# Leaving out the eleven filler products behind the first product of chunk 0's join

## The chip, the cores and the metric

The kernel runs on one core of a Trainium2 chip. The core has five engines that take instructions from queues of their own: PE (TensorE, matrix products; its weight loads are listed as PEld), DVE (VectorE), ACT (ScalarE), POOL (GpSimd) and SP (SyncE, which here only issues DMAs). The metric is the device time of one execution in microseconds. Before the change three runs took 508.95, 509.15 and 509.38 us, with a median of 509.15 us.

## The reference

A delta-rule attention over 4 batches, 8 heads, 768 positions of 48 channels, and behind it, on the heads put together to 384 channels, a layer norm and an MLP with a residual:

```python
k_n = k / (np.linalg.norm(k, axis=-1, keepdims=True) + 1e-06)
for t in range(S):
    kt, vt, bt = (k_n[:, :, t], v[:, :, t], beta[:, :, t, None])
    y[:, :, t] = np.einsum('bhd,bhde->bhe', q[:, :, t], state)
    v_old = np.einsum('bhde,bhd->bhe', state, kt)
    state = state + bt[:, :, :, None] * np.einsum('bhd,bhe->bhde', kt, vt - v_old)
...
xn = (x - mu) / np.sqrt(var + 1e-06) * g_ln
ch = np.maximum(xn @ w_ch1, 0.0) @ w_ch2
return (x + ch).astype(np.float32)
```

Inputs and output are float32, apart from the two weight matrices, which reach the kernel as float64 and are converted there to float32.

## The kernel before

**Tiling.** The 768 positions are cut into 12 chunks of 64. Within a chunk the recurrence is solved as a triangular system. Its inverse is made on DVE: `rows_inverse` (L823) does two chunks at a time by row elimination, a multiplication (L849) and a subtraction (L856) per row, 31 rows. Before it starts it scales the Gram matrix by `db_b`, which needs the inputs beta in `beta_b` (L834, L838), and POOL puts the diagonal into `xb` (L835). Chunk 0 has a way of its own that is done sooner: `rows_near` inverts blocks of 16 rows, and `near_join` (L801) joins two of them by two products on PE, both on line L812, each of 128 matmuls of 32 by 32. Between the two, ACT copies the first product's result with a sign (L815); after the second, DVE puts it into place (L819).

**The recurrence.** `recur(c)` (L875) computes for a chunk `u` in three products (L908) with an ACT copy into `u` after the first and the third (L914) and a DVE subtraction after the second (L912), then the outputs (L919, copied by ACT at L956), and the update of the state (L929, which ACT copies into `s_all` at L940 in chunk 0). The layer norm follows: statistics on DVE (L962, L963), the root on ACT (L968), scaling on DVE (L974), transposes on PE (L1006), and for chunk 0 the gain on ACT (L1022) and DVE (L1012). Products of the keys and queries with the state (L886) open the next chunk.

**The MLP.** `mlp(c)` multiplies the normed chunk by the two weight matrices. In chunks 0 to 2 the first matrix is done at L1184 and chunk 0's second at L1206; later chunks use schemes with fewer products (L1100, L1281). All of these are PE work, and from some 67 us on they fill PE.

**Loads.** SP issues nearly all loads in one queue, in the order of its instructions: keys (`kr`, `tb`), queries (`tb`), `v`, and beta in eight pieces. One that waits holds all behind it. The function that issues them is `dma` (L370; the trace names its line L373). ACT issues the loads of the weights, which ACT, DVE and POOL convert (L514, L519, L522, L532).

**Order.** The function records 2783 steps, each with its engine. `ORDER`, a tuple of step numbers, says in which order they are issued; `in_this_order` binds each engine to that order, and the DMAs of SP and ACT to one another. What a step waits for comes from the tiles that it reads and writes.

**The filler products.** `zeros` multiplies `nought` by a column of `nought` that is repeated 256 times, into columns of the PSUM bank `f0`; nothing reads the result:

```python
def zeros():
    nc.tensor.matmul(f_[0][:, 256:512], nought, nought[:, 0:1].to_broadcast([128, 256]))
for _ in range(WARM):
    add("PE", 0.44, zeros, FK[0], [], np=2, arr=0.44, name="warm", after=["nought"])
```

With `WARM = 26` these are steps 62 to 87; the trace names their line L1364. `nought` is the first 128 columns of the tile `u`. `Line.emit` asks of every step that the steps it depends on were issued before it, except for steps named "warm", which may stand anywhere or be left out. On the chip each is two weight loads and two matmuls, since a float32 product takes two passes.

Of the kernel before, what the change touches and what calls it, by code (L numbers as in the profile page):

```python
# [57 lines left out]
def pool(n):  # L58
# [13 lines left out]
    346, 72, 80, 86, 183, 64, 54, 203, 223, 123, 213, 179, 126, 191, 220, 206, 194, 215, 14, 226, 184, 202, 296, 297, 329, 328, 199, 219, 298, 227,  # L72
    82, 340, 228, 197, 710, 196, 208, 299, 62, 44, 198, 185, 331, 356, 343, 344, 385, 330, 386, 204, 192, 217, 300, 229, 231, 186, 230, 233, 234, 235,
    49, 83, 63, 347, 236, 221, 301, 302, 304, 303, 305, 360, 306, 322, 200, 307, 310, 187, 237, 238, 239, 240, 67, 65, 365, 323, 308, 311, 241, 309,
    313, 361, 391, 242, 243, 393, 312, 244, 245, 314, 246, 315, 247, 248, 249, 250, 363, 332, 390, 320, 335, 370, 251, 252, 253, 392, 188, 316, 362,
    317, 318, 319, 254, 388, 321, 846, 255, 256, 257, 258, 259, 232, 387, 571, 260, 364, 69, 844, 843, 740, 394, 568, 573, 569, 567, 395, 709, 708,
    704, 845, 743, 572, 741, 570, 566, 737, 366, 428, 261, 429, 336, 389, 337, 334, 338, 333, 397, 262, 263, 264, 265, 266, 367, 267, 268, 269, 270,
    271, 272, 273, 274, 275, 276, 357, 432, 433, 277, 396, 398, 436, 278, 279, 280, 281, 282, 283, 348, 284, 285, 286, 287, 288, 289, 290, 291, 292,
    293, 437, 440, 441, 430, 431, 371, 444, 375, 372, 445, 349, 294, 434, 435, 373, 295, 448, 449, 354, 368, 353, 352, 350, 438, 491, 359, 374, 369,
    452, 453, 439, 467, 468, 442, 454, 469, 470, 380, 399, 443, 492, 400, 455, 456, 490, 574, 471, 493, 494, 495, 496, 498, 497, 500, 401, 402, 472,  # L80
    457, 458, 403, 446, 404, 447, 381, 405, 501, 502, 503, 504, 505, 506, 507, 508, 509, 510, 511, 512, 513, 514, 706, 564, 742, 705, 711, 406, 720,
    563, 515, 516, 382, 517, 407, 717, 707, 716, 718, 715, 378, 713, 376, 377, 738, 719, 714, 736, 409, 383, 379, 1000, 351, 408, 473, 450, 474, 384,
    575, 518, 459, 712, 412, 410, 565, 413, 475, 476, 460, 411, 576, 1182, 461, 477, 721, 750, 739, 747, 1175, 746, 749, 751, 1176, 748, 752, 745,
    451, 414, 417, 418, 419, 577, 424, 415, 416, 420, 423, 421, 426, 462, 463, 519, 520, 478, 521, 522, 523, 579, 524, 525, 526, 479, 527, 528, 499,
    482, 483, 425, 422, 427, 578, 580, 581, 609, 582, 610, 615, 583, 584, 616, 585, 613, 586, 621, 529, 464, 622, 530, 611, 531, 484, 532, 533, 534,
    587, 535, 588, 536, 537, 538, 539, 540, 541, 542, 543, 722, 590, 614, 589, 726, 544, 545, 546, 547, 548, 549, 723, 753, 591, 627, 619, 728, 724,
    628, 727, 725, 550, 593, 485, 594, 612, 729, 734, 730, 620, 735, 642, 617, 731, 732, 618, 598, 733, 744, 551, 552, 486, 625, 643, 644, 645, 646,
    647, 754, 623, 626, 466, 841, 998, 592, 595, 624, 999, 755, 854, 850, 855, 848, 480, 849, 851, 997, 842, 481, 631, 1371, 1181, 599, 553, 554, 555,
    556, 600, 557, 488, 629, 1367, 853, 852, 1368, 633, 634, 759, 760, 756, 996, 632, 757, 487, 558, 559, 758, 652, 653, 654, 648, 605, 761, 893, 596,
    597, 489, 655, 630, 659, 660, 661, 656, 607, 762, 763, 766, 764, 606, 767, 636, 894, 639, 637, 635, 640, 638, 641, 895, 649, 856, 560, 765, 650,  # L90
    651, 1179, 465, 657, 662, 663, 667, 658, 664, 769, 601, 857, 669, 670, 671, 672, 673, 858, 674, 1004, 561, 1008, 1178, 1007, 1010, 1211, 1177,
    1005, 1009, 1003, 603, 602, 1001, 1006, 1180, 608, 770, 604, 771, 675, 562, 860, 859, 847, 684, 861, 772, 1002, 666, 897, 665, 773, 774, 668, 768,
    776, 775, 778, 779, 676, 685, 686, 687, 677, 678, 679, 680, 862, 688, 681, 780, 689, 781, 690, 901, 782, 783, 784, 785, 863, 682, 683, 864, 865,
    786, 1011, 787, 902, 907, 908, 788, 789, 866, 913, 867, 868, 870, 872, 871, 695, 696, 697, 698, 914, 699, 700, 903, 919, 790, 791, 792, 793, 794,
    795, 796, 797, 875, 904, 798, 799, 800, 920, 801, 802, 701, 803, 869, 804, 905, 805, 925, 906, 1012, 934, 935, 936, 937, 911, 876, 873, 874, 880,
    877, 912, 1013, 909, 917, 1014, 898, 899, 806, 878, 807, 881, 808, 809, 810, 811, 812, 813, 814, 815, 816, 918, 910, 915, 916, 923, 921, 926, 900,
    879, 882, 691, 928, 927, 896, 692, 931, 1208, 1188, 1476, 1207, 1190, 941, 1212, 1184, 694, 924, 929, 930, 1048, 1016, 944, 945, 946, 1015, 1017,
    922, 938, 939, 932, 933, 943, 942, 1050, 1051, 1018, 1052, 961, 1019, 940, 1373, 1473, 1185, 693, 703, 1187, 884, 1372, 1370, 817, 702, 1189, 883,
    885, 888, 887, 889, 886, 1191, 818, 819, 1183, 1632, 1366, 1186, 962, 820, 821, 1020, 947, 822, 951, 963, 964, 952, 953, 965, 948, 949, 1021, 950,
    823, 824, 825, 826, 969, 970, 892, 890, 891, 954, 966, 967, 955, 956, 971, 972, 968, 973, 976, 977, 978, 974, 1022, 1058, 1061, 1062, 1053, 959,  # L100
    1057, 1059, 1192, 827, 975, 1023, 1025, 1024, 979, 958, 960, 828, 957, 980, 1060, 1063, 981, 1065, 1049, 1064, 829, 830, 1026, 1193, 982, 1027,
    1030, 831, 832, 1031, 1035, 1066, 1215, 987, 1068, 1070, 1071, 1198, 1199, 1069, 1036, 1028, 1029, 1197, 833, 1037, 777, 988, 989, 990, 991, 992,
    1072, 1054, 1067, 1073, 1213, 984, 1194, 1032, 1033, 1034, 993, 1038, 1039, 834, 1074, 1195, 1196, 1200, 1201, 1202, 1203, 1206, 835, 836, 837,
    1075, 838, 1076, 1204, 1077, 1086, 1205, 1079, 1210, 1376, 1214, 1081, 1055, 1078, 839, 840, 1398, 1475, 1084, 1082, 1216, 1217, 1375, 1379, 1369,
    1377, 1040, 1633, 1378, 1471, 1080, 1095, 1041, 1083, 1044, 1085, 1087, 1089, 1056, 1096, 1090, 1635, 1636, 1380, 1042, 1218, 1043, 1219, 1220,
    1092, 1093, 1631, 1382, 1209, 1101, 1046, 1098, 1102, 1088, 1047, 1045, 1091, 1097, 1113, 1221, 1103, 1222, 1099, 1094, 1374, 1114, 1115, 1116,
    1117, 1223, 1118, 1225, 1381, 994, 1383, 1822, 995, 1828, 1100, 1472, 1667, 1637, 1642, 1224, 1119, 1384, 1388, 1385, 1249, 983, 985, 1252, 1253,
    1644, 1640, 1665, 986, 1248, 1104, 1107, 1108, 1250, 1389, 1105, 1110, 1254, 1120, 1109, 1123, 1124, 1125, 1126, 1386, 1387, 1390, 1130, 1256,
    1391, 1131, 1132, 1133, 1134, 1127, 1140, 1135, 1112, 1122, 1106, 1111, 1121, 1128, 1392, 1393, 1394, 1399, 1400, 1141, 1142, 1143, 1129, 1144,
    1148, 1401, 1402, 1145, 1403, 1477, 1149, 1136, 1251, 1255, 1137, 1138, 1150, 1151, 1152, 1153, 1404, 1406, 1405, 1408, 1146, 1154, 1257, 1258,  # L110
    1139, 1147, 1409, 1227, 1410, 1230, 1231, 1397, 1226, 1259, 1260, 1166, 1155, 1167, 1168, 1156, 1395, 1235, 1169, 1262, 1411, 1412, 1228, 1413,
    1414, 1229, 1157, 1158, 1159, 1236, 1415, 1416, 1160, 1264, 1170, 1261, 1232, 1263, 1417, 1266, 1396, 1478, 1237, 1418, 1419, 1420, 1233, 1265,
    1268, 1267, 1421, 1171, 1270, 1422, 1480, 1269, 1423, 1172, 1271, 1273, 1239, 1275, 1161, 1272, 1277, 1163, 1424, 1274, 1286, 1425, 1234, 1276,
    1278, 1280, 1479, 1287, 1238, 1426, 1481, 1482, 1281, 1427, 1282, 1428, 1429, 1430, 1431, 1432, 1288, 1283, 1284, 1289, 1292, 1293, 1483, 1304,
    1305, 1306, 1294, 1314, 1315, 1307, 1643, 1279, 1634, 1827, 1662, 1639, 1826, 1308, 1484, 1290, 1824, 1291, 1309, 1316, 1317, 1318, 1319, 1645,
    1641, 1928, 1825, 1295, 1296, 1433, 1434, 1630, 1638, 1407, 1240, 1162, 1173, 1435, 1298, 1436, 1437, 1438, 1241, 1242, 1299, 1301, 1439, 1440,
    1311, 1244, 1243, 1930, 1331, 1332, 1821, 1474, 1174, 1646, 1310, 1164, 1165, 1246, 1485, 1321, 1245, 1322, 1247, 1285, 1297, 1300, 1302, 1312,
# [1362 lines left out]
```

## Time and profile before

| | us |
|---|---|
| median of three runs | 509.15 (508.95 to 509.38) |
| the profiled execution | 509.78 |
| its span, first to last instruction | 508.1 |
| PE busy, PEld busy | 486.3, 438.4 |
| DVE, POOL, ACT busy | 388.0, 248.6, 186.4 |
| mean granted clock of PE | 0.985 of full |

The page gives the busy time of each engine over the whole span; the chain of waits goes back from the last instruction, at each step to what released it. In the chain, "issue" is time in which an engine waited for nothing that the profile shows. Times in microseconds count from the first instruction.

### The profile page before, as it was taken

How to read it: one execution, taken by the hardware profiler on the slowest of the kernel's cores; microseconds unless marked ns; L12 is line 12 of the kernel's file. 1: busy time of each engine (PE TensorE's matmuls, PEld its weight loads, DVE VectorE, ACT ScalarE, POOL GpSimd, SP SyncE). 2: the span in 40 equal slices, each digit the busy share in tenths (PEclk: the TensorE clock that was granted, in tenths of full speed). 3: DMA queues.
4: the chain of work that ended last, by engine and by line, in shares of the span. 5: the costliest groups of instructions: out<-in, count | busy, mean ns of one | idle time of the engine just before them, and what ended most of it. 6: DMA issues, size and time to landing. Idle time of an engine off the chain costs nothing.

```text
span 508.1 us, 21971 instructions
## 1 busy us (share of the span) xinstructions
PE 486.3 (96%) x9688; PEld 438.4 (86%) x9688; DVE 388.0 (76%) x855; ACT 186.4 (37%) x403; POOL 248.6 (49%) x377
## 2 busy tenths in 40 slices
PE   8668799999999999999999999999999999999996
PEld 5456686778898899999999989999999999999996
DVE  0865999989999967948999848999979889354241
ACT  2685544534512224442223434413431421424130
POOL 5036223302584588482291474391681671835554
PEclk9979899999999999999999999999999999999999
DMA  6995964532643432544234441620421303002011
GB/s 107 279 217 117 238 95 127 69 53 42 118 60 63 78 75 50 104 80 67 65 65 85 101 72 46 110 48 2 111 51 40 80 3 92 7 31 65 1 39 32
DMA packets 155855, 40.47 MB, mean 80 GB/s; under 512 B 149232, under 2 KB 152304, under 8 KB 155760
## 3 DMA queue, kind: packets, MB, share of 16 engines
q1 hardware_dynamic: 151760, 29.21, 31.5%
q10 hardware_dynamic: 3712, 9.83, 6.1%
q8 instruction: 76, 1.25, 1.0%
q14 instruction: 19, 0.16, 0.1%
q0 software_dynamic: 288, 0.03, 0.1%
HBM read 30.79 MB, written 8.26 MB: 77 GB/s over the span
## 4 chain that ended last, share of the span: by engine, by line
PE 79%; DVE 8%; DMA 4%; issue 3%; SPq 2%; ACT 2%; POOL 1%; DVEq 0%; ACTq 0%; POOLq 0%
PE f L1281 26%; PE f L1100 21%; PE f L1184 8%; PE two L908 5%; PE f L1206 3%; SPq L373 2%; PE two L886 2%; PE by L919 2%; PE two L680 2%; PE by L886 2%; DVE tmp L849 2%; PE f L1364 1%; PE two L929 1%; DVE xb L856 1%; DVE kq L577 1%
## 5 line engine op out<-in xcount | busy, mean ns | idle before, releaser
L1267 POOL TENSOR_TENSOR h_all<-h_all 128x256 f32<-128x256 f32 x99 | 75.1, 770 | 14.8 <-ACT h_all L1193 11.4
L1281 PE MATMUL f<-w_sb,h_all 128*128 128x192 f32 x396 | 81.3, 331 | 0.0
L849 DVE TENSOR_TENSOR tmp<-xb,gb 128x31 f32<-128x31 f32 (+15 forms) x186 | 76.8, 413 | 4.7
L1281 PE MATMUL f<-words,h_all 128*128 128x192 f32 x396 | 77.9, 331 | 0.6 <-DVE o L1299 0.6
L856 DVE TENSOR_TENSOR xb<-xb,tmp 128x31 f32<-128x31 f32 (+15 forms) x186 | 72.5, 390 | 3.7
L1113 DVE TENSOR_TENSOR h_all<-f,h_all 128x512 f32<-128x512 f32 x90 | 60.5, 684 | 17.6 <-PE f L1100 17.0
L1306 POOL TENSOR_TENSOR words<-h_all 128x128 f32<-128x128 f32 x66 | 30.5, 482 | 83.0 <-ACT h_all L1116 51.7
L1281 PEld LDWEIGHTS f<-words,h_all 128*128 128x128 f32 x396 | 65.2, 190 | 2.6 <-DVE o L1299 1.0
L1281 PEld LDWEIGHTS f<-w_sb,h_all 128*128 128x128 f32 x396 | 64.6, 190 | 1.7 <-issue 0.4
L1184 PE MATMUL f<-xnt,w_sb 128*128 128x256 f32 x216 | 51.3, 386 | 0.9 <-DVE xnt L1012 0.9
L1108 ACT COPY h_all<-f 128x512 f32<-128x512 f32 x36 | 21.1, 585 | 72.9 <-PE f L1100 28.7
L1184 PEld LDWEIGHTS f<-xnt,w_sb 128*128 128x128 f32 x216 | 39.8, 190 | 7.2 <-issue 1.2
L1100 PE MATMUL f<-kt,w_sb 128*128 128x128 f32 x360 | 45.7, 276 | 0.0
L1116 ACT ACTIVATE h_all<-h_all 128x512 f32<-128x512 f32 x54 | 32.1, 625 | 33.5 <-DVE h_all L1113 33.5
L1100 PEld LDWEIGHTS f<-kt,w_sb 128*128 128x128 f32 x360 | 43.3, 192 | 0.4 <-issue 0.2
L914 ACT COPY u<-two 128x768 f32<-128x768 f32 x24 | 19.1, 798 | 48.3 <-PE two L908 36.4
L1100 PE MATMUL f<-xnt,w_sb 128*128 128x128 f32 x288 | 35.0, 276 | 0.0
L1100 PEld LDWEIGHTS f<-xnt,w_sb 128*128 128x128 f32 x288 | 33.3, 192 | 0.3
L1281 PE MATMUL f<-w_sb,words 128*128 128x192 f32 x132 | 28.1, 330 | 0.0
L1083 POOL TENSOR_TENSOR kt<-xnt,kt 128x128 f32<-128x128 f32 x9 | 4.1, 455 | 48.4 <-PE f L1100 48.4
L1193 ACT ACTIVATE h_all<-f 128x256 f32<-128x256 f32 x36 | 13.7, 384 | 37.1 <-PE f L1184 32.1
L532 POOL TENSOR_TENSOR w_sb<-words 128x768 uint32<-128x768 uint32 (+1 forms) x9 | 12.2, 1364 | 28.6 <-DVE words L519 14.3
(201 smaller groups left out, 885.8 us busy)
## 6 DMA issues: line engine op xcount, KB each, us to landing
words<-in_moe_w_ch_dram ACTq DMA_DIRECT2D x8, 768.0 KB, 5.2
v<-in_v_dram SPq DMA_DIRECT2D x24, 192.0 KB, 4.4
kr<-in_k_dram SPq DMA_DIRECT2D x46, 96.0 KB, 3.5
out_dram<-o SPq DMA_DIRECT2D x46, 96.0 KB, 2.4
xld<-xlt SPq DMA_DIRECT2D x9, 384.0 KB, 2.5
xnt<-xld SPq DMA_DIRECT2D x36, 96.0 KB, 2.7
tb<-in_q_dram SPq DMA_DIRECT2D x40, 64.0 KB, 2.8
tb<-in_k_dram SPq DMA_DIRECT2D x32, 64.0 KB, 3.6
```

The source lines that it names most:

```text
L849: lambda j=j, n=n, w=w, t=t: nc.vector.tensor_tensor(out=t, in0=xb[:, 0:n, j : j + 1].to_broadcast([128, n, w]), in1=gb[:, j : j + 1, j + ...
L856: "DVE", dve(n * w), lambda t=t, rest=rest: nc.vector.tensor_tensor(out=rest, in0=rest, in1=t, op=ALU.subtract),
L886: nc.tensor.matmul(dst[half(e), hp, j], src[drows(hp), (e if n else key_half(c, hp, e)) * GP + j], s_all[drows(hp), e, j], start=(n == 0 o ...
L908: nc.tensor.matmul(*args(e, e ^ hp, 2 * j + hp))
L1100: nc.tensor.matmul(wide(p[:, 128 * n : 128 * n + 128]), w[:, 128 * n : 128 * n + 128], r, start=start and n == 0, stop=True, skip_group_ch ...
L1108: add("ACT", act(512), lambda: nc.scalar.copy(to[0], ps(p)), pk, to[1])
L1113: add("DVE", dve(512), lambda: nc.vector.tensor_tensor(out=to[0], in0=in0, in1=in1, op=op), [*pk, *y[1]], to[1])
L1116: add("ACT", act(512), lambda: nc.scalar.activation(to[0], to[0], ACTF.Relu), [], to[1])
L1184: nc.tensor.matmul(p[:, 0:TOK], w1_sb[:, t, f * 128 : (f + 1) * 128], xnt[:, t], start=(t == 0), stop=(t == KC - 1))
L1267: add(eng, cost, lambda: e.tensor_tensor(out=out_, in0=x, in1=y, op=op), r, w, port=2 if eng == "Pool" else 1)
L1281: lambda f=f, t=start and f == 0: nc.tensor.matmul(p[:, 0:D2], lhs(f), rhs[:, f], start=t, stop=(f == F2 - 1), skip_group_check=True),
L1306: lambda f=f + i: e.tensor_tensor(out=s3[f], in0=one(0, 0)[0](f), in1=one(1, 0)[0](f), op=ALU.subtract),
```

## The change

Of the 26 filler products eleven are left out: the three between the two products of chunk 0's join, one behind the second, two behind the second product of `u`, two behind the third, two behind the update of the state, and one ahead of the product of chunk 1's keys and queries (L643). The fifteen before the join's first product stay. Nothing else changes: the remaining 2772 steps have the same order. In the tuple, the places are these (pieces of its lines, each with the numbers around):

```diff
 ORDER = (
...
-    327, 43, 342, 45, 346, 72, 80, 86, 183, 64, 54, 203,
+    327, 43, 342, 45, 346, 183, 54, 203,
...
-    298, 227, 82, 340, 228, 197, 710, 196, 208, 299, 62, 44,
+    298, 227, 340, 228, 197, 710, 196, 208, 299, 44,
...
-    234, 235, 49, 83, 63, 347, 236,
+    234, 235, 49, 347, 236,
...
-    239, 240, 67, 65, 365, 323,
+    239, 240, 365, 323,
...
-    260, 364, 69, 844, 843,
+    260, 364, 844, 843,
```

Of the neighbours, 183 is the join's second product, 298 and 300 the second and third product of `u`, 44 a load of beta, 710 the load of keys that SP issues ahead of it, 323 the copy of the state, 364 a conversion of weights.

On PE the sequence of instructions changes like this, and on the other engines it stays the same:

```diff
 L812 Matmult f2<-xn1,kt3 32x32 x64
-L1364 Matmult f0<-u 128x256 x3
 L812 Matmult f3<-xt3,xn1 32x32 x64
-L1364 Matmult f0<-u 128x256
 L908 Matmult two<-v0,xt3 32x48 x32
 L555 Matmult f3<-ident,tb2 128x128 x4
 L555 Matmult f2<-ident,tb2 128x128 x4
 L908 Matmult two<-u,goff 32x48 x32
-L1364 Matmult f0<-u 128x256 x2
 L908 Matmult two<-v0,xt3 32x48 x32
-L1364 Matmult f0<-u 128x256 x2
 L919 Matmult two<-u,pt0 64x48 x16
 L919 Matmult by<-u,pt0 64x48 x16
 L929 Matmult two<-u,kr0 64x48 x32
-L1364 Matmult f0<-u 128x256 x2
 L555 Matmult two<-ident,tb1 128x128 x4
...
 L1006 Matmult by<-ident,xln 128x128 x6
-L1364 Matmult f0<-u 128x256
 L643 Matmult two<-qt1,kq0 64x64 x32
```

## The prediction

> **What bounds the kernel now.** I read the page's totals first, then the chain of waits of the stretch in which the eleven products stand, then the waits, and last PE's busy time in stretches of one clock step.
>
> ```profile
> PE 486.3 (96%) x9688; PEld 438.4 (86%) x9688; DVE 388.0 (76%) x855; ACT 186.4 (37%) x403; POOL 248.6 (49%) x377
> ...
> q8 instruction: 76, 1.25, 1.0%
> ```
>
> PE is busy for 96% of the span, so what leaves it can count in full, where PE ends last. The queue q8 is the instruction stream: 76 packets, 1.25 MB, 16.4 KB each. PE's 9688 matmuls and 9688 weight loads with some 105 semaphore instructions make 64 bytes each of that, so one packet holds 256 PE instructions.
>
> The chain of waits from 31 to 47 us (start, us, what):
>
> ```profile
> 31.31 0.94 PE f L812 x61
> 32.24 3.16 issue
> 35.40 0.76 PE f L812 x32
> 36.16 2.77 PE f L1364 x6
> 38.93 1.23 PE f L812 x95
> 40.16 0.63 PE f L1364 x2
> 40.80 0.23 issue
> 41.03 0.88 PE two L908 x63
> 41.91 1.04 PE f L555 x8
> 42.95 0.02 issue
> 42.97 0.31 SPq L373
> 43.28 0.04 issue
> 43.32 2.09 DMA beta_b<-in_beta_dram
> 45.41 1.43 issue
> 46.84 0.20 DVE db_b L834
> ```
>
> L1364 are the fillers: 2.77 us of three and 0.63 of a fourth lie on the chain. Behind them it leaves PE, by way of SP and a DMA, for DVE's row elimination (L834, then L849 and L856), which leads until DVE's L659 ends at 66.57 and PE's L886 starts at 66.6. From there PE leads, to the end in the main. So the head is worth what it moves L834.
>
> The 3.16 us of "issue" at 32.24 stand in the middle of one product: after 88 of its 128 pairs of weight load and matmul, where nothing is waited for. In the trace's records that is PE instruction 1217. PE halts again at instruction 1729 (42.91 to 43.12) and 1985 (46.10 to 47.12, between two fillers): 1217 + 2 x 256 and 1217 + 3 x 256. So these are limits of blocks, and PE waits for q8. q8's packets ended at 33.94, 41.88 and 45.73; PE went on 1.47, 1.24 and 1.39 us later. A packet starts after PE has passed the limit before, in the head 0.8 to 2.2 us after. From 39.55 to 43.12 and from there to 47.12, PE got 256 instructions in 3.6 and 4.0 us and could not have had them sooner.
>
> Two of the waits:
>
> ```profile
> DVE xt L819 <- PE f L812: 2.0, 1, 2.0
> ACT u L914 <- PE f L1364: 2.0, 1, 2.0
> ```
>
> The second says that a filler holds up real work: `nought`, which it reads, is a part of `u`, so ACT's copy into `u` waits until it has read.
>
> PE by stretches of 3.41 us (window, length, busy PE, PEld, DVE, ACT, POOL, then granted clock, DMA share, GB/s):
>
> ```profile
> 28.47:31.89 3.42, 2.11 (x134) 1.63 (x134) 0.94 (x2) 3.38 (x7) 0.00 (x0) 1.00 0.92 292
> 31.89:35.30 3.41, 0.35 (x43) 0.26 (x30) 3.41 (x10) 3.32 (x7) 0.37 (x1) 1.00 1.15 172
> 35.30:38.71 3.41, 3.31 (x47) 2.47 (x46) 1.81 (x3) 2.47 (x6) 3.41 (x3) 0.50 0.71 145
> ...
> 45.54:48.95 3.41, 2.10 (x71) 1.22 (x59) 2.08 (x4) 1.14 (x2) 1.78 (x2) 1.00 0.73 132
> ...
> 59.19:62.61 3.42, 2.50 (x73) 2.03 (x72) 3.32 (x8) 2.04 (x5) 1.20 (x1) 1.00 1.02 282
> ```
>
> The granted clock goes in such steps. It is half for one step after a step in which PEld was busy for 1.22 us or less, and full after 1.63 (1.54 at the least, from 11.41 to 14.82). Between 1.22 and 1.54 the trace doesn't decide.
>
> **The change, part by part.** Eleven fillers go: 22 matmuls and 22 weight loads, 44 PE instructions. No other engine loses or gains one, and no DMA moves in its queue.
>
> Three behind the first product of the join. The second product needs ACT's L815, which ended at 36.83, so it could start at 36.93 instead of 38.86. Its clock is still half: 41 pairs took 0.46 us at 35.41, 11.3 ns each. With 12 instructions fewer in front, the next block limit comes after 87 of its 128 pairs, at 37.9. The block isn't there: q8's packet ran from 37.35 to 38.27, released at 35.41, before the change takes hold; with 1.24 us that is 39.5. (Before, PE passed this limit at 39.55, so the packet was already all but the limit.) The last 41 pairs take 0.35 us at 8.5 ns (47 pairs from 39.55 to 39.95), or 0.46 at half clock, and 0.2 to drain: the product ends between 40.05 and 40.2, before 40.16. I take -0.1. Bounds: -1.55, if the fetch did not hold (36.93 + 128 x 11.3 ns + 0.2 = 38.6), and +0.1.
>
> The fourth, at 40.09, lies beside DVE's L819, 40.21 to 40.93, for which L908 waits: nothing. Without that cover it is worth 0.63.
>
> Four around the second and third product of `u`. Two fill PE's wait for DVE's L912: nothing; without L912, 1.1 us. Two were split by the halt at 1985, and ACT's L914 started at 47.86 only; now it can at 46.0, when L908 has ended. `u`, the products L919 and the update L929 come 1.8 us earlier, L929 perhaps more (it ran at half clock). Hidden: ACT's copy of the state, L940, stands in ACT's queue behind L968, which waits for DVE's L963, done at 53.73. SP's load of kr0, which waited for L929 until 52.2, goes some 2 us earlier with the loads of v behind it; the first user of that v is POOL at 65.17.
>
> Two at 52.32 fill PE's wait for L940: nothing. The last, at 59.59, pushed L643 by 0.4 us; its user, DVE's L659, starts at 65.35 in DVE's own order: nothing.
>
> L834 needs beta_b. Fifteen of its sixteen parts were in by 45.31, the last at 46.76, behind q8's packet of 44.77 to 45.73. Both hang on PE: SP issues this load behind one that waits for L555, and the packet follows PE's passage of 1729. If both move by -0.1, so does L834. Bounds: -1.4, where they miss each other (DVE is free at 45.40), and +1.0, where L555 runs at half clock (eight transposes at 0.21 us instead of 0.11, 0.85 more) and still meets the packet.
>
> The clock. From 59.19 to 62.61 PEld loses 2 x 0.19 and has 1.65, over 1.54: full, as before. From 38.71 to 42.13 some 1.5 us is left (41 pairs, L908, a part of L555): undecided. If the step from 62.61 went to half, L1184 and L886 would end at 67.3 instead of 66.6: +0.7. I take 0.
>
> The Trainium skill (TensorE: Matmul & The Clock Gate, section "HAM oscillation — how this bites in real kernels") speaks against the change: PE gaps of more than some 3.4 us bring half the clock. The step that followed 45.54 to 48.95 disagrees in this: its longest gap was 1.5 us and the clock still fell, so the share of a step decides. By its rule the only new step at half would follow the gap before 55.23, where the clock was half already, and the sum would not change. The same skill (Runtime: NRT & Kernel Launch, section "Instruction fetch mechanics") gives blocks of 16 KiB, 256 instructions, which the trace bears out, and calls crossing a block limit mostly hidden; by that the sum would be the -1.55 above.
>
> All later block limits move by 44 instructions. After 60 us none halted PE before; the nearest had 0.1 us to spare (219.78). With the limits moved, the tightest block (375.6 to 377.5, L929 and L919, 256 instructions in 1.9 us) could wait up to 1.0 us, if q8 is released only as L929 starts; if the reading ahead seen elsewhere (packets up to 1.9 us before the passage) holds, nothing. I take 0.
>
> Sum: -0.1 us. The profiled execution took 509.78 for a span of 508.1, 0.6 over the median of 509.15; set against the median, 509.05.
>
> **The rivals.** *The chain is believed*: the fetch doesn't hold the second product, or the beta_b load misses the packet. For it: 2.77 + 0.63 us on the chain. Against it: the three halts 256 instructions apart. It gives 509.15 - 1.4 to 1.55 = 507.7; over -1.0 it counts as faster. *The clock falls*: without fillers PE runs at half from 38.7 to 45.5 and from 62.6 to 66. L555 then delays beta_b by up to 1.0 and L1184 PE's start by 0.7: 510.85; it decides from PEld under 1.2 to 1.5 us in the steps before. For it: four half steps already, each after a thin step; against it: 1.65 in the step that matters most. *A moved block limit halts PE* around 377: 510.1, seldom more.
>
> **How the numbers follow.** No change, 509.0: 0.48 (from -0.7 to +0.9). The chain: 0.20. The clock: 0.24. The block limit: 0.08, half of it inside 0.2%. A measurement tells 0.2%, 1.0 us, from no change. Faster 0.20, same 0.52, slower 0.28. The range, 507.5 to 510.9, takes in the chain's bound and the clock's.
>
> **What would show it.** Right: PE halts inside the second L812 product near 38 and goes on at 39.5; L914 runs near 46; L834 within 0.3 us of 46.84; L886 near 66.6. Wrong: that product done by 38.7; beta_b in by 45.5; half clock after 62.6; a PE "issue" near 375.

## The result, and the profile after

The changed kernel takes 512.8 us (median of 13 runs, 511.4 to 514.93). The kernel before, run beside it on the same chip, takes 509.95 us (13 runs, 508.95 to 513.06). The ratio is 1.0043, with a 95% interval of 1.0024 to 1.0063 (the plain quotient of the two medians is 1.0056). It is slower by 0.43%, some 2.2 us; on the 509.15 us that the prediction started from, that is 511.3, above the range of 507.5 to 510.9. The likeliest case, no change, did not come true.

The profiled execution of the changed kernel took 512.5 us for a span of 510.8 us, 2.7 us more than the span before. Its page begins like this:

```profile
span 510.8 us, 21927 instructions
PE 483.4 (95%) x9666; PEld 437.0 (86%) x9666; DVE 389.1 (76%) x855; ACT 186.0 (36%) x403; POOL 249.1 (49%) x377
```

PE has 2.9 us less work (486.3 before) and yet ends 2.7 us later: it stands idle 5.6 us longer. The timeline of PE shows where (start, us, engine, line, operation, tiles, number of matmuls; in brackets the idle time before it and what ended it). Before the change, from 50 to 65 us:

```profile
50.27 2.12 PE L929 MATMUL two<-u,kr 64*64 64x48 f32 x64
...
55.23 0.65 PE L555 MATMUL two<-ident,tb 128*128 128x128 f32 x4 [1.77 <-ACT s_all L940]
55.82 2.03 PE L608 MATMUL f<-kt 48*32 48x64 f32 x128
57.78 1.11 PE L555 MATMUL two<-ident,tb 128*128 128x128 f32 x4
58.69 1.07 PE L1006 MATMUL by<-ident,xln 128*128 128x128 f32 x6
59.59 0.60 PE L1364 MATMUL f<-u 128*128 128x256 f32 x2
60.12 1.16 PE L643 MATMUL two<-qt,kq 48*64 48x64 f32 x64
62.20 1.53 PE L1184 MATMUL f<-xnt,w_sb 128*128 128x256 f32 x6 [0.92 <-DVE xnt L1012]
63.67 1.15 PE L886 MATMUL by<-s_all,qt 48*64 48x48 f32 x64
```

After it:

```profile
36.05 1.39 PE L812 MATMUL f<-xt,xn 32*32 32x32 f32 x87 [0.69 <-ACT xn L815]
38.75 0.79 PE L812 MATMUL f<-xt,xn 32*32 32x32 f32 x41 [1.31 <-issue]
40.40 1.50 PE L908 MATMUL two<-v,xt 32*32 32x48 f32 x64 [0.86 <-POOL w_sb L532]
41.83 1.97 PE L555 MATMUL f<-ident,tb 128*128 128x128 f32 x8
...
50.63 1.92 PE L929 MATMUL two<-u,kr 64*64 64x48 f32 x64
55.87 1.12 PE L555 MATMUL two<-ident,tb 128*128 128x128 f32 x4 [3.32 <-ACT s_all L940]
56.92 2.03 PE L608 MATMUL f<-kt 48*32 48x64 f32 x128
...
59.55 0.71 PE L1006 MATMUL by<-ident,xln 128*128 128x128 f32 x5
61.75 0.27 PE L1006 MATMUL by<-ident,xln 128*128 128x128 f32 x1 [1.49 <-issue]
61.95 1.16 PE L643 MATMUL two<-qt,kq 48*64 48x64 f32 x64
63.68 1.53 PE L1184 MATMUL f<-xnt,w_sb 128*128 128x256 f32 x6 [0.57 <-POOL w_sb L532]
65.14 1.07 PE L886 MATMUL by<-s_all,qt 48*64 48x48 f32 x57
66.53 0.33 PE L886 MATMUL by<-s_all,qt 48*64 48x48 f32 x7 [0.32 <-issue]
66.79 1.56 PE L1184 MATMUL f<-xnt,w_sb 128*128 128x256 f32 x6
68.28 1.15 PE L886 MATMUL two<-s_all,kq 48*64 48x48 f32 x64
```

Three halts "<-issue" stand in the middle of a group of like matmuls, where nothing is waited for. The first is the one that the prediction named: the second product of the join, after 87 pairs. The other two were not there before. Between the matmul ahead of the halt in L1006 and that ahead of the halt in L886 lie 256 PE instructions, so these are block limits, 2497 and 2753 in the prediction's count of PE instructions (1217 + 5 x 256 and 1217 + 6 x 256). Before, 2497 fell into L608 (57.38 us) and 2753 into L886 (64.15 us), with the blocks in hand 2.4 and 4.7 us ahead; now the packets of q8 that carry the blocks ended at 60.33 and 64.99, 1.4 and 1.5 us before PE went on. The limit ahead of them, 2241, had come at 51.83 in L929, ahead of PE's wait for the state (L940); now it comes behind that wait, at 56.96 in L608. From there to limit 2497 PE takes 3.0 us instead of 5.5, and the block's packet begins only 2.5 us after limit 2241. The L886 group that started PE's dense stretch at 66.62 starts at 68.28: +1.67 us.

L834, which the prediction watched, moves from 46.84 to 47.48. The chain of waits says why (start, us, what):

```profile
40.40 1.50 PE two L908 x64
41.90 1.91 PE f L555 x8
43.83 0.31 SPq L373
44.19 2.51 DMA beta_b<-in_beta_dram
46.70 0.79 issue
47.48 0.20 DVE db_b L834
```

L555 takes 1.91 us where it took 1.04. It runs at half clock, as PE's busy time by clock step shows (window, length, busy PE, PEld, DVE, ACT, POOL, then granted clock, DMA share, GB/s):

```profile
35.40:38.81 3.41, 1.45 (x91) 1.32 (x95) 2.59 (x2) 3.39 (x8) 3.07 (x3) 0.50 0.84 226
38.81:42.22 3.41, 2.55 (x107) 2.33 (x108) 2.12 (x5) 0.74 (x2) 2.63 (x4) 0.50 0.51 94
42.22:45.64 3.42, 3.02 (x72) 2.50 (x70) 0.18 (x1) 3.42 (x7) 1.67 (x2) 0.50 0.14 19
45.64:49.05 3.41, 1.67 (x72) 1.48 (x72) 2.58 (x5) 1.01 (x2) 1.24 (x2) 0.50 0.49 77
...
62.70:66.12 3.42, 2.85 (x92) 2.28 (x83) 3.01 (x9) 1.85 (x4) 1.14 (x2) 1.00 0.86 123
```

Five steps in a row are half now, from 35.4 to 52.5 us; before, it was the one from 35.3 to 38.7 and the one from 49.0 to 52.4. Behind 100 us the changed kernel loses another 1.5 us in steps, each at such a halt: 0.46 at 160 us (L919), 0.5 at 297 (L1281), 0.4 and 0.16 at 365 to 381. Some 0.5 us come back near 230 us, where the kernel before was held up in its profiled execution, so that 1.04 us is left. The kernel before had no such halt behind 60 us.

So there are two suspects. **Theory L**: 44 PE instructions fewer move every later block limit, and limits now fall where PE reaches them before the block is there. **Theory C**: without the fillers the clock falls to half in the head, L555 is longer, beta_b and L834 come later, and PE's dense stretch starts late. (The expectations of the first four kernels were written before these two letters were set; where they use letters of their own, the mechanism that they name says which is meant.)

### The profile page after: what moved, and what is told of

It is laid out like the page before. It is cut to its first block, busy times and chain, and to the rows that moved or that the text cites. A ratio compares the mean times of both kernels' runs of the same rounds, so it can differ in the third digit from the quotient of the medians.

```text
span 510.8 us, 21927 instructions
## 1 busy us (share of the span) xinstructions
PE 483.4 (95%) x9666; PEld 437.0 (86%) x9666; DVE 389.1 (76%) x855; ACT 186.0 (36%) x403; POOL 249.1 (49%) x377
## 4 chain that ended last, share of the span: by engine, by line
PE 79%; DVE 8%; POOL 5%; issue 3%; ACT 3%; SPq 1%; DMA 1%; POOLq 0%; DVEq 0%
PE f L1281 28%; PE f L1100 20%; PE f L1184 8%; PE two L908 5%; PE f L1206 3%; PE by L886 2%; PE by L919 2%; PE two L680 2%; PE two L886 2%; DVE tmp L849 2%; PE two L929 2%; DVE h_all L1113 1%; SPq L373 1%; DVE xb L856 1%; POOL h_all L1267 1%
## 5 line engine op out<-in xcount | busy, mean ns | idle before, releaser
L1281 PE MATMUL f<-w_sb,h_all 128*128 128x192 f32 x396 | 81.5, 331 | 0.7 <-ACT h_all L1116 0.3
L1281 PE MATMUL f<-words,h_all 128*128 128x192 f32 x396 | 77.7, 331 | 0.0
L1281 PEld LDWEIGHTS f<-w_sb,h_all 128*128 128x128 f32 x396 | 64.6, 190 | 2.7 <-issue 1.0
L1281 PEld LDWEIGHTS f<-words,h_all 128*128 128x128 f32 x396 | 65.2, 190 | 1.7 <-issue 0.6
L1184 PE MATMUL f<-xnt,w_sb 128*128 128x256 f32 x216 | 51.3, 386 | 0.6 <-POOL w_sb L532 0.6
L1184 PEld LDWEIGHTS f<-xnt,w_sb 128*128 128x128 f32 x216 | 39.8, 190 | 6.8 <-POOL w_sb L532 0.7
L1281 PE MATMUL f<-w_sb,words 128*128 128x192 f32 x132 | 28.1, 330 | 0.0
```

The source lines that it names most:

```text
L1184: nc.tensor.matmul(p[:, 0:TOK], w1_sb[:, t, f * 128 : (f + 1) * 128], xnt[:, t], start=(t == 0), stop=(t == KC - 1))
L1281: lambda f=f, t=start and f == 0: nc.tensor.matmul(p[:, 0:D2], lhs(f), rhs[:, f], start=t, stop=(f == F2 - 1), skip_group_check=True),
```

## The experiments

In every kernel all that the reference asks for is computed. Only fillers, whose results nothing reads, are left out, made smaller or moved, and in some a load is issued earlier. Every ratio is to the kernel before, run on the same chip. Step numbers are those of the order in the code.

**Thin fillers in their places.** The eleven fillers become products of a 32x32 weight with 8 columns: as many PE instructions as before, so the same block limits, but hardly any work.

```diff
+    def thin():
+        nc.tensor.matmul(f_[0][0:32, 256:264], nought[0:32, 0:32], nought[0:32, 0:1].to_broadcast([32, 8]))
...
-        add("PE", 0.44, zeros, FK[0], [], np=2, arr=0.44, name="warm", after=["nought"])
+        add("PE", 0.44, thin if len(line.steps) in THIN else zeros, FK[0], [], np=2, arr=0.44, name="warm", after=["nought"])
```

> The eleven fillers stay in their places as four PE instructions each, but with a 32x32 weight tile and 8 columns, so that they do next to no work. The block limits of PE's instruction stream are those of the kernel before; the clock has to fall as in the changed kernel (half from 35 to 52 us). Theory A (two causes: the half clock delays beta_b and L834 by about 0.6 us, the moved block limits cost the rest of the 2.2 to 2.7 us): 0.3 to 0.9 us over the kernel before, no halt inside L1006 near 60 and no halts at 160, 297 and 365 us. Theory B (the clock alone costs it, the halts only fill time that was lost anyway): 2 to 2.7 us over the kernel before.

Measured: 509.51 us, ratio 0.999 (0.9972 to 1.0008). Nothing is lost, where both theories had a loss, though the clock was half from 33.8 to 64.5 us, longer than in the changed kernel. The clock alone does not cost the time. (This profiled execution was some 2 us late already at the end of the join's first product; two more follow below.)

**Thin fillers all in one wait.** The changed kernel, with the eleven thin products ahead of step 365, where PE waits for the state.

```diff
-    239, 240, 365, 323,
+    239, 240, 72, 80, 86, 64, 82, 62, 83, 63, 67, 65, 69, 365, 323,
```

> The changed kernel, with eleven such thin fillers all put where PE waits for the copy of the state (52.5 to 55.8 us). Up to there everything is the changed kernel, its block limits too; behind it the limits are those of the kernel before. Theory A: L834 at about 47.5 as in the changed kernel, but PE's L886 at 67.2 instead of 68.3 and no later halts: 0.4 to 1.0 us over the kernel before. Theory B: as the changed kernel, 2 to 2.7 us over.

Measured: 511.4 us, ratio 1.0037 (1.0015 to 1.006). It should have given the time back and did not. Its trace has PE halt 0.32 us among the thin products (limit 2241) and 0.56 us in L608 (limit 2497), though 2497 stands within two pairs of where it stood before the change: PE gets past limit 2241 2.6 us later than before, and the next packet begins at 56.91 instead of 54.09. Then the clock is half to 69.5 us, through the start of the dense stretch. A limit's place is not enough; when PE passes the limit before counts as well.

**The last part of beta_b first.** SP issues step 44, the load that L834 waits for, ahead of step 710, which waits for PE's L555; once on the kernel before and once on the changed one.

```diff
-    197, 710, 196, 208, 299, 62, 44, 198,
+    197, 44, 710, 196, 208, 299, 62, 198,
```

> The kernel before, fillers and all; on SP the last load of beta is issued ahead of the load of keys that waits for PE's L555, not behind it. The path from PE to DVE's L834 through SP is gone. Both theories put that path in front of L834: beta_b is in by 45.4 and L834 starts at 45.4 to 45.5 instead of 46.84, and PE's L886 at 65.2 instead of 66.6; 1.0 to 1.4 us under the kernel before. If something else is late next (the keys of the load put behind, or POOL), 0 to 0.5 us under.

> The changed kernel with the same load moved. The half clock can then delay L834 only through L912 (46.4) and L519: L834 at 46.8. Theory A: the halts stay, about 0.7 us less than the changed kernel, 1.3 to 2.0 us over the kernel before. Theory B (all of the loss comes from the clock by way of beta_b): within 0.5 us of the kernel before.

Measured on the kernel before: 508.42 us, ratio 0.9981 (0.9959 to 1.0003), with L834 at 45.38 (-1.46). On the changed kernel: 514.19 us, ratio 1.0084 (1.0055 to 1.0112). There L834 starts at 46.32, earlier than the 46.84 before the change, and the loss is not smaller (the two intervals overlap, so that it is larger is not shown). So the loss does not need L834's lateness: with L834 in time, PE's halt in L1006 (1.04 us) and half clock from 63.2 to 66.7 us still have the second L886 group start 1.87 us late.

**Thin fillers early.** The changed kernel, with the thin products ahead of step 112, in a PE wait at 21 to 24 us, ahead of the join. From 60 us on the limits then stand as before the change.

```diff
-    56, 112, 324,
+    56, 72, 80, 86, 64, 82, 62, 83, 63, 67, 65, 69, 112, 324,
```

> The changed kernel, with eleven tiny products (32x32 weight, 8 columns) put at about 21 us, in PE's wait ahead of the transposes at 23.8 us. They give PE's instruction stream back its 44 instructions ahead of the join, so from 60 us on its block limits fall where they fell before the change; the clock of the head stays as in the changed kernel, mostly half. Theory L (the moved block limits cost the time): no halt in L1006 or L886 between 58 and 67, and the halts after 150 us are gone; ratio to the kernel before 0.999 to 1.002. Theory C (the lower clock of the head costs it, through L555, beta_b and L834, or through the half steps between 59 and 69): the loss stays, 1.003 to 1.006.

Measured: 510.13 us, ratio 1.0 (0.9978 to 1.0021). The loss is gone, as theory L has it, with the clock at half from 33.0 to 60.3 us. (In the head this kernel's limits lie elsewhere too, and one of them halts PE for 1.46 us ahead of L555 at 42.11.) PE's timeline in the stretch of the two halts:

```profile
56.31 2.03 PE L608 MATMUL f<-kt 48*32 48x64 f32 x128
58.27 1.11 PE L555 MATMUL two<-ident,tb 128*128 128x128 f32 x4
59.18 1.35 PE L1006 MATMUL by<-ident,xln 128*128 128x128 f32 x6
60.46 1.16 PE L643 MATMUL two<-qt,kq 48*64 48x64 f32 x64
62.24 1.53 PE L1184 MATMUL f<-xnt,w_sb 128*128 128x256 f32 x6 [0.62 <-DVE xnt L1012]
63.71 1.15 PE L886 MATMUL by<-s_all,qt 48*64 48x48 f32 x64
```

No "issue" is left in these lines; L1184 waits 0.62 us for DVE, as it waited 0.92 before the change. This kernel also gains something that does not belong to the question: the halt in the join's first product took 0.64 us instead of 3.16, since q8's packet came at 30.68 instead of 32.46 us.

**Wide fillers.** The other way round: fillers as long as before, with fewer instructions. Eleven pairs of fillers of 256 columns each become one of 512 columns, in the place of the first named: 76 and 71, 87 and 78, 84 and 68, 66 and 85, 70 and 79, 74 and 77 ahead of the join; 72 and 80, 64 and 86, 82 and 62, 83 and 63, 67 and 65 behind it. That is 44 instructions fewer.

```diff
+    def wide():
+        nc.tensor.matmul(f_[0], nought, nought[:, 0:1].to_broadcast([128, 512]))
```

> The kernel before, in which eleven times two fillers of 256 columns become one of 512 columns: PE is as long at fillers as before, with 44 instructions fewer. Six of the merged pairs stand ahead of the join, five behind it, so behind 60 us the block limits stand where the changed kernel has them, while the clock is kept up. Theory L: PE halts at about 59 to 61 us in L1006 for 0.5 to 1.5 us, and later at about 160, 297 and 365 as in the changed kernel; ratio 1.002 to 1.005. Theory C: nothing is lost, 0.999 to 1.001.

Measured: 512.67 us, ratio 1.0044 (1.0016 to 1.0072), the same loss as that of the changed kernel, with all the filler time still there. The halt at limit 2497 is here too; it fell into the filler behind L1006:

```profile
60.95 0.82 PE L1006 MATMUL by<-ident,xln 128*128 128x128 f32 x6
61.61 0.38 PE L1364 MATMUL f<-u 128*128 128x256 f32 x1
63.42 0.38 PE L1364 MATMUL f<-u 128*128 128x256 f32 x1 [1.43 <-issue]
```

And the later gaps in PE's weight loads, from the start of one to the start of the next, come at the same work as in the changed kernel: 0.73 us in L919 at 162.7, 0.56 in L1281 at 299.6, 0.58 in L1281 at 367.6 (there 0.41, 0.82 and 0.58). It is no clean proof against theory C, though: the clock was half here too for a part of the time (34.6 to 41.4, 48.2 to 58.5 and, behind the halt, 65.3 to 68.7), and L834 came at 48.32.

**Only the last three out, only the first eight out.** The kernel before without steps 67, 65 and 69, or without the other eight. Behind 60 us the limits move by 12 or by 32 instructions.

> The kernel before without the last three of the eleven fillers (two at 52.3, one at 59.6 us). Block limits move by 8 to 12 instructions only: limit 2497 stays in L608, no halt there. Theory L: no change, 0.999 to 1.001. Theory C: with less PE work from 52 to 60 us the step from 59.2 or 62.6 us may fall to half the clock, L1184 and L886 then end up to 0.7 us later; 1.000 to 1.0015.

> The kernel before without the first eight of the eleven fillers; the last three (52.3 and 59.6 us) stay. Block limits behind 60 us move by 32 instructions. Theory L: limit 2497 falls four matmuls earlier than in the changed kernel, at the end of L555 or the start of L1006, and PE halts there by 0.5 to 1.5 us; of the later halts that at 160 us stays or goes with the place: ratio 1.001 to 1.004. Theory C (the clock): the last three fillers keep the step from 59 us up, and little is lost, 0.999 to 1.001.

Measured without the last three: 510.0 us, ratio 0.9997 (0.9974 to 1.002). Without the first eight: 514.82 us, ratio 1.0088 (1.0056 to 1.012), twice the loss of leaving out all eleven. Both theories had it smaller. The number of fillers left out does not decide; the place of the limit differs. PE's timeline without the first eight:

```profile
59.87 0.42 PE L1006 MATMUL by<-ident,xln 128*128 128x128 f32 x1
63.01 1.22 PE L1006 MATMUL by<-ident,xln 128*128 128x128 f32 x5 [2.72 <-issue]
64.03 1.06 PE L1364 MATMUL f<-u 128*128 128x256 f32 x2
65.02 1.99 PE L643 MATMUL two<-qt,kq 48*64 48x64 f32 x64
66.93 2.93 PE L1184 MATMUL f<-xnt,w_sb 128*128 128x256 f32 x6
69.79 1.79 PE L886 MATMUL by<-s_all,qt 48*64 48x48 f32 x64
```

The limit lies four matmuls earlier, and PE halts 2.72 us there, as q8's packet ran from 60.49 to 61.59 only. L1184 then takes 2.93 us instead of 1.53, at half clock. The steps of the clock say what the halt did (columns as above):

```profile
61.00:64.40 3.40, 1.39 (x6) 1.35 (x6) 1.86 (x5) 0.13 (x1) 1.49 (x1) 0.50 0.99 283
64.40:67.80 3.40, 3.40 (x68) 2.58 (x67) 2.48 (x7) 1.56 (x4) 0.00 (x0) 0.50 0.43 47
67.80:71.20 3.40, 3.40 (x57) 2.48 (x60) 3.30 (x8) 1.23 (x3) 1.59 (x1) 0.50 0.75 109
71.20:74.60 3.40, 3.40 (x95) 2.82 (x89) 3.19 (x9) 1.75 (x5) 0.00 (x0) 0.99 0.74 102
```

The halt thins the step from 61.0 (PE busy for 1.39 us), and two more at half follow, now in the stretch that PE bounds. That the halt kept the clock down here is not shown, since it was half before the halt as well. Clearer are the kernels in which the step with the halt at limit 2497 ran at full clock: with PEld at 1.41 and 1.32 us in that step (changed, beta_b first, the execution above and one below) and at 1.49 (wide fillers) the step behind it was half; with 1.59 and 1.77 (changed, the first and a second execution) it stayed full. So a halt can be paid a second time, through the clock.

**Thin fillers at 81 us.** The changed kernel, with the thin products (into the bank `f2`) ahead of step 467, the second group of L1206. The head keeps its moved limits, all behind 81 us stands as before the change.

> The changed kernel with the eleven tiny products at about 81 us, in PE's wait for the diagonal ahead of the second pair of L1206. Block limits up to there stand as in the changed kernel, behind it as before the change. Theory L: the halts in L1006 and L886 at 60 to 67 us stay and with them some 1.0 to 1.7 us; the halts at 160, 297, 365 and 380 us (0.41, 0.82, 0.50, 0.28 in the changed kernel) are gone: 1.001 to 1.003, and by the trace the shift against the kernel before stays where it is at 100 us instead of growing by 1.6 us. Theory C: all of the loss stays, 1.004, and the shift at 100 us does not grow in either kernel but for noise, so the halts behind it cost nothing.

Measured: 513.53 us, ratio 1.006 (1.0036 to 1.0083), more than theory L had. The thin products were not hidden: PE is later by 1.0 us from there on. But the trace tells the two stretches apart: L886 starts 2.75 us late, 3.75 us are reached at 95 us, and then the lateness does not grow (3.19 at the end); no gap of over 0.25 us at a limit is left behind 85 us.

**Fillers early or in place, and beta_b first.** Can both kernels be beaten? Three tries: thin fillers in their places and step 44 first; thin fillers early and step 44 first; and step 44 first on the kernel before a second time.

> The kernel before with the eleven fillers as tiny products in their places, and with the load of the last part of beta_b issued on SP ahead of the load that waits for PE's L555. Both theories: the limits stand as before, beta_b no longer waits for L555 at half clock, so DVE's L834 starts at 45.4 to 45.9 instead of 46.8 and the end comes 1.0 to 1.8 us earlier: 0.9965 to 0.998. If half clock in the head costs by itself, it gains less than 0.5 us, 0.999 or more.

> The changed kernel with the eleven tiny products at about 21 us and, besides, the load of the last part of beta_b issued on SP ahead of the load that waits for PE's L555. Theory L: limits from 60 us on stand as before the change, so no halt in L1006, L886 or later, and L834 starts at 45.4 to 46.0 instead of 46.84: 0.9965 to 0.999. Theory C: the half clock keeps its loss and the load only takes some of it back: 1.000 to 1.003.

> The kernel before with only the load of the last part of beta_b issued earlier on SP, a second time, to narrow its interval: 0.997 to 0.9995 by both theories, with L834 near 45.4 us and no halt behind 60 us, since no PE instruction moves.

Measured: 0.9981 (0.9959 to 1.0004), 0.9992 (0.9973 to 1.0011) and 0.9999 (0.9971 to 1.0028). None is told from the kernel before; the 0.19% of the first run of the earlier load did not repeat. In the first of the three L834 came at 46.92, not at 45.4 to 45.9 as both theories had it, though beta_b was in by 42.13. The chain of waits leads there from L555, at half clock to 44.14, over the load of keys that waits for it (tb, landed at 46.63) and DVE's L519: the earlier load of beta does not free L834 from L555. The last one's trace shows a thing of its own. All PE instructions stand as before the change, and L834 starts at 45.56; yet PE halts 2.18 us at limit 2497, in L608, for q8's packet began at 56.41 instead of 54.09:

```profile
54.99 1.91 PE L608 MATMUL f<-kt 48*32 48x64 f32 x117
59.09 0.44 PE L608 MATMUL f<-kt 48*32 48x64 f32 x11 [2.18 <-issue]
```

In the first run of this kernel PE halted there too, for 0.94 us, without a loss. The packet comes with a spread, so with the limit in its old place PE can still halt now and then (in the two traces of the kernel before it did not); with the limits of the changed kernel it halted in every execution seen.

**More executions.** What is there each time, and what by chance? The changed kernel twice more, the kernel before once, thin fillers in place twice, and the changed kernel with step 44 first once.

> The changed kernel itself, a second execution under the profiler. Theory L: the halt in L1006 at block limit 2497 is there again, by 0.5 to 3 us as q8's packet comes, and the halts near 160, 297, 365 and 380 us with 0.2 to 0.9 us each. Open: whether the clock from 62 to 69 us is full, as in the first profile (then L886's second group is late by 1.2 to 2 us), or half, as in the kernel that had the same head (then by 2.5 to 4).

> The changed kernel, a third execution. As for the second: a halt in L1006 every time by theory L; by theory C no steady halt, and lateness only where the clock is half behind 62 us.

> The kernel before, a second execution. Theory L: limit 2497 lies in L608 near 57.4 us, where the packet was in 2.4 us ahead in the first profile; a halt there only if the packet is released 2 us later than then. Full clock from 62 us, no halt of over 0.2 us behind 60 us, span 506 to 510.

> The kernel before with the eleven fillers as tiny products in their places, a second execution (the first was profiled in its slowest run, 2 us late already at the join). Theory L: PE takes some 5.1 us from limit 1473 to limit 1729 at half clock, as in the changed kernel, so L834 is late by 0.5 to 1.5 us, but no limit halts PE from 55 to 70 us, and nothing is added behind it: span 507 to 510. Theory C: L834's lateness is all of the loss, and where it is 1 us late the end is 1 us late or more.

> The same kernel, a third execution: no halt behind 55 us by theory L, and the end not later than L834 against the kernel before; theory C as for the second.

> The changed kernel with the load of the last part of beta_b issued first, a second execution: L834 is not late (45.5 to 47 us), so what the end loses comes behind it. Theory L: the halt in L1006 is there again (0.3 to 2.5 us), with half clock behind it where that step is thin, and the later halts of 0.2 to 0.9 us; span 511 to 514. Theory C: with L834 in time the loss is under 1 us but where the clock is half from 62 us.

Single times of these: 513.64, 514.17, 509.70, 510.50, 509.19 and 513.14 us. Beside the first three the kernel before took 508.39 us, beside the last three 513.01, so single times tell no two of these kernels apart; the traces do more. Their traces and the earlier ones, each against the first profile of the kernel before, in us: how late L834 starts, how much of lateness is added from there to the second L886 group (66.62 before), and how much from there to PE's last product.

| execution | L834 | to L886 | to the last product | sum |
|---|---|---|---|---|
| changed, first | +0.64 | +1.03 | +1.04 | +2.7 |
| changed, second | +1.61 | +0.45 | +1.87 | +3.9 |
| changed, third | +3.54 | +0.33 | +0.56 | +4.4 |
| changed, beta_b first, first | -0.52 | +2.39 | +1.14 | +3.0 |
| changed, beta_b first, second | -0.10 | +2.67 | +0.87 | +3.4 |
| first eight out | +1.32 | +5.06 | +1.35 | +7.7 |
| wide fillers | +1.48 | +2.36 | +1.22 | +5.1 |
| before, second | +0.34 | 0.01 | -0.41 | -0.1 |
| before, beta_b first, first | -1.46 | 0.01 | -0.84 | -2.3 |
| before, beta_b first, second | -1.28 | +3.09 | -0.68 | +1.1 |
| last three out | -0.26 | 0.01 | +0.31 | +0.1 |
| thin in place, first | +2.73 | 0.02 | -0.70 | +2.0 |
| thin in place, second | +0.38 | 0.02 | +0.38 | +0.8 |
| thin in place, third | -0.09 | 0.02 | -0.52 | -0.6 |
| thin early | +0.03 | 0.02 | -0.17 | -0.1 |
| thin in place, beta_b first | +0.08 | 0.02 | -0.66 | -0.6 |
| thin early, beta_b first | -0.85 | 0.01 | -1.00 | -1.8 |

The two groups part in the third and fourth column. With the limits moved (the upper seven), 0.33 to 5.06 us are added between L834 and L886, and 0.56 to 1.87 behind it, 1.15 on average. With the limits behind 60 us in place or within 12 instructions of it (the lower ten), nothing is added before L886, but for the one late packet, and -0.43 on average behind it (so the first profile of the kernel before was itself some 0.4 us behind the others there). So the moved limits cost some 1.6 us behind 67 us on average, and the two groups do not overlap there (0.56 at the least, 0.38 at the most), though not by much. The two kernels with thin products in a wait or at 81 us, whose limits are moved in one part and not in the other, are left out of the table; with their limits back in place they lie between the groups (+0.41 and +0.45; the second has its 1.0 us at 81 us in it). The halts themselves tell the groups apart better: behind 85 us PE and its weight loads stand still at one to three limits for 0.12 to 0.51 us each in every trace of the upper seven, and at no limit for over 0.07 us in the thirteen others. Ahead of it there are two ways to be late, and the larger hides the other: the later L834, the less the halt in L1006 adds. The three executions of the changed kernel reach L886 1.67, 2.06 and 3.87 us late; with L834 in time, the halt and the half clock behind it make it 1.87 and 2.57. Not all of this is the change's: the end of the join's first product, ahead of all that the change touches, came 0.76 us early in the first of the three and 0.62 and 1.74 late in the others.

## Why the prediction was wrong

**What held.** The halt inside the second product of the join came as written, at 87 pairs, and in the first execution ended at 38.75 instead of 39.5; the join ended early there and nothing came of it. The chain's 2.77 and 0.63 us of fillers were worth nothing. L834 hung on L555 and on q8's packet as described: in six executions it started 1.1 to 1.3 us after that packet had ended (46.84 after 45.73, 47.48 after 46.22, 48.45 after 47.19, 50.38 after 49.12, 47.18 after 45.87, and 48.26 after 47.06 in the kernel with the same head). In these the sixteenth part of the load landed 1.1 to 1.6 us after the fifteenth; with thin fillers in place, where the packet was over before the first part landed, 0.02 us or less after it. Behind 62.6 us the clock was full in the first two executions, and in the third from 63.6.

**What failed: "All later block limits move by 44 instructions ... I take 0."** Of this term the prediction looked for one tight place, near 377 us, with a price of at most 1.0 us. It missed the head, where the spare time of limit 2497 was 2.4 us less the 1.4 that a landed block needs until PE goes on. Moved by 44 instructions, limit 2241 falls behind PE's wait for the state and limit 2497 into L1006. Between the two PE runs through L608, L555 and most of L1006 faster than the block comes: 1.49, 0.90 and 0.38 us of halt in the three executions. At 160, 297 and 365 to 381 us the same happens on a smaller scale, together 1.5 us in the first profile. The place near 377 was one of these: it cost 0.17 us at 380 in the first profile, the least of all, and 0.72 in the changed kernel's first execution with beta_b first. The prediction also took the fetch for quicker than it is: its "0.8 to 2.2 us after" leaves out the packet that held up the join, which began at 32.46, 3.3 us after PE had passed limit 961 at 29.14. Thin fillers early or in place (1.0 and 0.999) against wide fillers (1.0044) and eight out (1.0088) show that it is the limits.

**The second miss: "-0.1" for L834.** It measured +0.64, +1.61 and +3.54, of which 0.62 and 1.74 us in the second and third stood ahead of the change (the first was 0.76 early there). Its mechanism was in the text as a rival and as a bound of +1.0 (L555 at half clock, still meeting the packet); the step from 38.81 ran at half, behind one with PEld at 1.32 us, and although it came to 2.33 us itself, half clock went on to 52.5. From limit 1473 to 1729 PE took 5.17 us in each of the three executions instead of 3.4, so the packet behind 1729, which holds up beta_b, came later by up to 3.4 us. The bound counted L555 alone, not L908 and the packet behind it. That this is not the clock alone is seen from thin fillers in place: the same stretch takes 5.1 us there, and L834 was late by 0.38 and -0.09 us, because that packet began 0.65 us ahead of PE's passage and 0.17 behind it (43.75 and 43.69 us). In the changed kernel it began 1.3 us behind it in all three executions (45.26 in the first). How far ahead of PE the fetch reads is not settled here. (One reading was off without bearing on the sum: the longest gap of 1.5 us that the prediction names from 45.54 to 48.95 runs from the start of one weight load to that of the next; the idle time in it is 1.29 us.)

**The rivals.** "The clock falls" had the right place and near the right time (510.85), but its first half cost nothing where the limits were in place (thin fillers in place), and its second half, half clock behind 62.6 us, did not come in the changed kernel's first two executions. "A moved block limit halts PE" was the right mechanism at 0.08, in the wrong place and at 1.0 us of the 2.2 measured. No rival had the moved limits and the later L834 together.

**Whether crossing a limit is hidden.** The Trainium skill (Runtime: NRT & Kernel Launch, section "Instruction fetch mechanics") calls the cost of crossing a block limit mostly hidden. By it the change would have gained; here it cost 0.38 to 2.72 us at limit 2497 alone, in the kernels with that limit moved. The twenty traces agree with "mostly": of 1480 limits that PE passed behind 22 us, 76 brought a halt of 0.1 us or more. What decides is when the block's packet ends: at the 66 halts of 0.3 us or more PE went on 1.2 to 1.7 us after that end, and no limit that it reached over 1.4 us after it brought a halt of 0.1 us. The time since the limit before does not decide by itself. Of 151 blocks that passed in under 3.6 us, 112 brought no such halt, and with a late packet PE lost 2.18 us after a block of 6.1 us (beta_b first, the second run).

## What to carry to other kernels

Count the instructions as well as the time: an edit that removes work also moves every block limit behind it. A limit that lay ahead of a wait can so come to lie behind it, and the next limit is then reached before its block is there; the place to look at is where PE reaches a limit within some 1.4 us of the end of the block's packet. To tell work and count apart, keep the count and take away the work (tiny products in place), and keep the work and take away the count (wide products); here one change of each kind told what the trace of the changed kernel alone left open. A profile of one execution is not the kernel: the same program had L834 at 47.5, 48.5 and 50.4 us.

## What was not expected of the hardware

A halt of the instruction fetch can be paid twice: with the changed limits and beta_b first, 1.04 us of halt in L1006 left the step from 59.8 us with 1.41 us of PEld, and in the step of half clock that followed six matmuls of L1184 took 2.54 us instead of 1.53. At half clock, more work does not bring full clock back as the steps before the change suggested: in the changed kernel, PEld at 2.33 and 2.50 us of 3.41 was followed by half clock, 2.93 and 3.34 by full; without the first eight, 2.58 by half and 2.48 by full. PEld's busy time does not decide the way back. And half clock can last for 30 us of the head (33.8 to 64.5) without a loss that the runs can tell (0.999, 0.9972 to 1.0008).
